# A transformer layer with adaptive layernorm: the attention gate's columns on GpSimd and VectorE instead of TensorE, its rows by way of DRAM, and four edits of order

## The chip, the core and the metric

The kernel runs on one core of one Trainium2 chip. TensorE (PE, with its weight loads shown as PEld) multiplies 128x128 weights with a moving tile of up to 512 columns into PSUM, eight banks of 512 fp32 columns on 128 partitions. VectorE (DVE), ScalarE (ACT) and GpSimd (POOL) work on SBUF, the first two on PSUM too. Nearly all transfers, among them the transposing ones ("turns"), are issued in order by SyncE (SP), and the FFN's gate and up weights by ScalarE. Each engine has its own instruction stream and waits on semaphores. The metric is the device time of one execution in microseconds (us), given as the median of several runs.

## The reference

Sequence 2048, model width 1024, 32 query heads and 4 key/value heads of width 128, a window of the last 512 keys, FFN width 3584, inputs in bf16. Six modulation vectors of 1024 come from a condition `c`.

```
mod = silu(c) @ w_mod                      # [1, 6*1024]: sa, ca, ga, sb, cb, gb
h = layernorm(x) * (1 + ca) + sa
q = h @ wq                                 # 32 heads
o = softmax(q @ k.T / sqrt(128)) @ v       # last 512 keys, 8 query heads per key head
x = x + ga * (o @ wo)
h = layernorm(x) * (1 + cb) + sb
out = x + gb * ((silu(h @ w_gate) * (h @ w_up)) @ w_down)
```

The change concerns `ga` (the attention gate: its 1024 values and the row of them that multiplies the attention output), the row of `gb`, the row of `silu(c)` that the later modulation columns are made with, and some of the order.

## The kernel before

All work is written from one Python body through a tracker (`T.op`), which knows the last writer and the readers of each buffer and puts the needed semaphore waits in front of an instruction. So the order on every engine is the order of the code, and nothing is reordered later. SBUF is one arena in which stages share space by hand; a new use of a region absorbs the waits of the old one.

**Opening (to L742).** x is loaded in chunks of 512 rows (4 tiles of 128). Chunk 0 is normalized and turned by PE. The columns of `ca` and `sa` are made on PE by products with one moving column (`mod_mm`, into bank XB = 7), and heads 0 to 7 of chunk 0 are projected before `sa` is known. `q_raw` keeps these projections in fp32, `q_bias_mm` makes the missing `sa @ wq` per head on PE, and `q_shifted` (L666) adds it. `shift` (L671) adds `sa` to chunk 0 for all later heads. Keys are turned by four PE transposes per key head (`k_turn`) and evicted by `k_evac`, the first in the opening, the others in steps 2, 4 and 6.

**Attention (L839 to L912).** A loop over `i` runs over 4 chunks x 32 heads. One step issues on PE: the query projection of head i + 3 (eight 512-column products into bank QB, evicted at L640; half a projection in steps 1 to 8), the scores of head i - 1 (four 512-column products, two exponentials on ScalarE), and the product with the values of head i - 2 (16 products of 129 columns). VectorE takes the reciprocal of the sums (L775), multiplies (L778), and SP turns the result into `oT_all`. `run_bg(1)` then advances a list of background tasks by one turn: `ln_task`, the layernorm of a later chunk (statistics at L415, powers on GpSimd at L420 and L422, `norm` at L426, an SP turn, `modulate` at L431), and `row_task`. Loads are issued at fixed steps: `LOADO` (output weights), `LOADX`, `load_wq`, `LOADT`. When a chunk's heads are done, `oproj` runs eight output pieces of 32 products, each followed by `resid` (L797, L799) with the gate's row `rowb[0]`.

**The gate.** `load_wga` brings the 1024x1024 part of `w_mod` in two halves (steps 2 and 3). In steps 7 (four weight chunks) and 9 to 12 (one each) `mod_mm` makes the 8 columns of `ga` on PE, 8 products of one column for each chunk. `row_task` turns columns into a row on all partitions: GpSimd makes diagonal tiles (L600), PE multiplies ones by four of them into XB, VectorE evicts (L608); twice. It runs three times: for `ga` from step 12, for `silu(c)` from step 17, and for `gb` once the 24 later columns are done. These later columns are made by VectorE (`mod_col`, L585) from SP turns of `w_mod` and the row of `silu(c)`.

**FFN (L915 on).** For each chunk 28 pairs of gate and up products, then `down`: eight pieces of 512 columns (the last of chunk 3 is two of 256), `resid` with `rowb[1]` and a store.

Of the kernel before, what the change touches and what calls it, by code (L numbers as in the profile page):

```python
# [3 lines left out]
ALU = mybir.AluOpType  # L4
# [3 lines left out]
P = 128  # L8
# [122 lines left out]
def bass_adaLN_cond__sliding_block_cached__swiglu_ffn__prompt_kernel(  # L131
# [53 lines left out]
    c6 = S_("c6", [P, DT], F32)  # L185
    mcol = S_("mcol", [P, 3 * DT], F32)
    gain = [S_("gain%d" % i, [P, DT], BF16) for i in range(2)]
# [24 lines left out]
    B_ident = _Buf("ident"); B_ones = _Buf("ones"); B_zw = _Buf("zw")  # L212
    B_diag = [_Buf("diag%d" % i) for i in range(4)]
    ident = arena.at(OFF_H20, [P], BF16, [B_ident])
    ones_bf = arena.at(OFF_H20 + 256, [P], BF16, [B_ones])
    diag = [arena.at(OFF_H20 + 512 + 256 * i, [P], BF16, [B_diag[i]]) for i in range(4)]
# [17 lines left out]
    B_cT = _Buf("cT"); B_sc = _Buf("sc"); B_late = [_Buf("late%d" % i) for i in range(4)]; B_c6 = _Buf("c6"); B_mcol = _Buf("mcol"); B_scr = _Buf("scr")  # L234
# [23 lines left out]
    with nc.Block() as block:  # L258

        @block.gpsimd  # L260
        def _(g):
# [32 lines left out]
            T.op(POOL, lambda: g.memset(ones_bf, 1.0), writes=[B_ones])  # L294
            T.op(POOL, lambda: g.memset(mhalf[:, :], -0.5), writes=[B_mh])
            T.op(POOL, lambda: g.memset(zwarm, 0.0), writes=[B_zw])  # L296

# [205 lines left out]
            T.op(ACT, lambda: A.activation(sc_bf[:, :], bank_bf(XB)[:, 0:DT], AF.Silu), writes=[PB[XB], B_sc])  # L503
            T.op(ACT, lambda: A.activation(acc[:, 0:1], mhalf[:, 0:1], AF.Exp), reads=[B_mh], writes=[B_acc])
# [54 lines left out]
            GCOLS = [(j, j) for j in range(DT)]  # L559

# [33 lines left out]
            def row_task(dst, dbuf, src, sbuf):  # L594
                T.op(POOL, lambda: g.tensor_copy(c6[:, :], src), reads=[sbuf], writes=[B_c6])

                def diags(n):
                    for q in range(4):
                        col = 4 * n + q
                        T.op(POOL, lambda: g.tensor_scalar(diag[q], ident, c6[:, col:col + 1], None, op0=ALU.mult),  # L600
                             reads=[B_ident, B_c6], writes=[B_diag[q]])

                diags(0)
                yield
                for n in range(2):
                    for q in range(4):
                        mm(bank(XB, P, q * P), ones_bf, diag[q], q == 0, q == 3, [B_ones, B_diag[q]], PB[XB], skip=True)
                    T.op(DVE, lambda: V.tensor_copy(dst[:, n * 512:(n + 1) * 512], bank(XB)),  # L608
                         writes=[PB[XB], dbuf])
                    if n == 0:  # L610
                        diags(1)
                    yield


# [117 lines left out]
            q_raw(6)  # L732
            mod_sa(3)
            T.op(DVE, lambda: V.tensor_copy(mod_bf[:, 0:DT], psap(XB * 512, [[2, DT]])), writes=[PB[XB], B_mode])
            qproj_mm(7, QB0[7], 0, HK)
            q_bias_mm(0, 2, BB)
            q_shifted(0)
            qproj_mm(7, QB0[7], HK, DT)
# [8 lines left out]
            oT_all = arena.at(OFF_OT, [Hq, CH], BF16, B_oT)  # L747

# [79 lines left out]
            def add_ln2(ch):  # L828
                s = ch % 2
                if ch == 0:  # L830
                    finish(rows)
                    h2s[0] = arena.at(OFF_H20, [DT, CH], BF16, B_h2[0])
                ln2[ch] = ln_task(ch, h2s[s], B_h2[s], 1, 3 * DT, B_late[1])
                bg.append(ln2[ch])

            LOADX = {19: 2, 40: 3}
            LOADT = {Hq + 2 + (9 * n) // 4: n for n in range(NL)}
            LOADO = {5 + (21 * p) // 8: p for p in range(8)}
            for i in range(1, NA + 2):  # L839
# [11 lines left out]
                for gk in {2: (1,), 4: (2,), 6: (3,)}.get(i, ()):  # L851
                    k_turn(gk, XB)
                    kd, ks = k_evac(gk, XB)
                    T.op(DVE, lambda: V.tensor_copy(kd, ks), writes=[PB[XB], B_kT[gk]])  # L854
                    if gk == Hkv - 1:
                        for b_ in B_hT[1]:
# [205 lines left out]
```

## Time and profile before

| | |
|---|---|
| median of 3 runs | 1274.79 us (1274.72 to 1275.56) |
| profiled execution | 1274.48 us, its span 1272.6 us |
| PE busy | 1259.1 us of the span |
| VectorE / ScalarE / GpSimd busy | 479.6 / 341.5 / 42.0 us |
| one-column products on PE from `sc_bf` | 192, of which 64 for the gate |
| row products on PE, 128x128 | 24, 2.3 us busy |
| HBM read and written | 119.54 MB, 4.19 MB |

The span is the time from the first to the last recorded instruction. "Busy" is the union of an engine's instructions; matmuls overlap, so the duration of one in the timeline is longer than the distance between two. In a line of the timeline the columns are start, duration (both us), engine, line, operation, output <- inputs, shapes and count; brackets at the end give the idle time before it and what ended it. Lines that a helper issues carry the helper's number: all products stand at L268, all PE transposes at L272.

### The profile page before, as it was taken

The numbers are of one execution on the slowest core, as the hardware profiler recorded it, in microseconds if no ns is written. First come the engines' busy times: TensorE is split into PE (matmuls) and PEld (weight loads), VectorE is DVE, ScalarE is ACT, GpSimd is POOL, SyncE is SP. The second block draws the span as 40 slices with busy tenths as digits, with TensorE's granted clock in tenths as the row PEclk, the third lists the DMA queues.
The fourth block names the chain that finished last, engine by engine and source line by source line (L and its number), as shares of the span: only waits on it lengthen the run. The fifth ranks groups of instructions, "written<-read, shape, count | busy, mean of one in ns | idle before, by whom it ended". The sixth has DMA issues, their size and how long they took to land.

```text
span 1272.6 us, 17800 instructions
## 1 busy us (share of the span) xinstructions
PE 1259.1 (99%) x7541; PEld 645.7 (51%) x7683; DVE 479.6 (38%) x897; ACT 341.5 (27%) x388; POOL 42.0 (3%) x102
## 2 busy tenths in 40 slices
PE   8999999999999999999999999999999999999999
PEld 5655545555455564455544444444444444444444
DVE  4655315764147651365322321233212331222122
ACT  4655204554025550155510111011100111011100
POOL 1020000000000010000000000000000000000000
PEclk9999999999999999999999999999999999999999
DMA  9999304886028641055353973055411644035200
GB/s 317 276 227 220 96 1 90 191 168 132 1 43 186 136 108 34 5 130 121 65 145 99 289 226 114 25 157 149 153 54 61 187 141 133 17 123 159 66 9 25
DMA packets 235854, 155.31 MB, mean 122 GB/s; under 512 B 129024, under 2 KB 222080, under 8 KB 235776
## 3 DMA queue, kind: packets, MB, share of 16 engines
q1 hardware_dynamic: 177520, 95.45, 31.2%
q10 hardware_dynamic: 58256, 58.73, 14.6%
q8 instruction: 60, 0.98, 0.3%
q14 instruction: 18, 0.15, 0.0%
HBM read 119.54 MB, written 4.19 MB: 97 GB/s over the span
## 4 chain that ended last, share of the span: by engine, by line
PE 98%; issue 1%; DVE 1%; POOL 0%; POOLq 0%
PE ps L268 98%; PE ps L272 0%; DVE arena L671 0%; DVE arena L666 0%; DVE rl L775 0%; DVE arena L778 0%; DVE arena L640 0%; DVE st L415 0%; POOL arena L296 0%; DVE tmp L797 0%; DVE arena L799 0%; DVE arena L487 0%; DVE arena L854 0%; POOL arena L291 0%; DVE bq L661 0%
## 5 line engine op out<-in xcount | busy, mean ns | idle before, releaser
L268 PE MATMUL ps<-arena 128*128 128x512 bf16 (+2 forms) x7236 | 1251.7, 333 | 10.3 <-POOL arena L408 2.2
L268 PEld LDWEIGHTS ps<-arena 128*128 128x128 bf16 x7378 | 635.5, 98 | 618.7 <-issue 2.2
L757 ACT ACTIVATE arena<-ps 128x1024 bf16<-128x1024 f32 x256 | 261.9, 1023 | 349.6 <-PE ps L268 337.8
L991 ACT ACTIVATE arena<-ps 128x512 bf16<-128x512 f32 x112 | 66.9, 597 | 506.4 <-PE ps L268 506.4
L992 DVE TENSOR_TENSOR arena<-ps,arena 128x512 bf16<-128x512 f32 x112 | 77.4, 691 | 276.6 <-PE ps L268 276.6
L797 DVE TENSOR_TENSOR tmp<-ps,rowb 128x512 f32<-128x512 f32 (+1 forms) x65 | 44.4, 683 | 318.8 <-PE ps L268 318.8
L640 DVE CAST arena<-ps 128x512 bf16<-128x512 f32 x120 | 82.9, 691 | 52.3 <-PE ps L268 52.3
L778 DVE TENSOR_TENSOR arena<-ps,rl 128x512 bf16<-128x512 f32 x128 | 88.5, 691 | 4.7 <-DVE rl L775 0.3
L775 DVE RECIPROCAL rl<-ps 128x4 f32<-128x4 f32 x128 | 23.3, 182 | 119.0 <-PE ps L268 118.9
L415 DVE BATCH_NORM_STATS2 st<-x_res 128x6 f32<-128x512 bf16 x62 | 42.3, 683 | 3.5 <-DMA x_res<-in_A_x_dram 3.4
L420 POOL TENSOR_SCALAR rstd<-mv 128x1 f32<-128x1 f32 x28 | 6.3, 226 | 887.2 <-DVE mv L419 887.2
L585 DVE SCALAR_TENSOR_TENSOR arena<-arena 128x1024 bf16<-128x1024 bf16 x24 | 29.1, 1214 | 0.0
L799 DVE TENSOR_TENSOR arena<-tmp,x_res 128x512 bf16<-128x512 f32 (+1 forms) x33 | 22.3, 675 | 1.1
L799 DVE TENSOR_TENSOR x_res<-tmp,x_res 128x512 bf16<-128x512 f32 x32 | 22.1, 692 | 1.1
L431 DVE TENSOR_SCALAR arena<-arena,gain,mod_bf 128x512 bf16<-128x512 bf16 x56 | 20.3, 405 | 0.0
L426 DVE TENSOR_SCALAR nsc<-x_res,mv,rstd 128x1024 bf16<-128x1024 bf16 x30 | 16.0, 534 | 0.0
L422 POOL TENSOR_TENSOR rstd<-rstd,mhalf 128x1 f32<-128x1 f32 x28 | 15.8, 563 | 2.3
L600 POOL TENSOR_SCALAR arena<-arena,c 128x128 bf16<-128x128 bf16 x24 | 14.4, 616 | 32.7 <-PE ps L268 32.4
L268 PEld LDWEIGHTS ps<-sc_bf,arena 128*128 128x128 bf16 x192 | 6.7, 96 | 2.6 <-DMA arena<-in_w_mod_dram 0.3
L268 PE MATMUL ps<-sc_bf,arena 128*128 128x1 bf16 x192 | 6.8, 163 | 0.1
L419 DVE BATCH_NORM_AGGREGATE mv<-st 128x2 f32<-128x12 f32 x28 | 5.8, 208 | 1.0
L653 DVE COPY arena<-ps 128x512 f32<-128x512 f32 x4 | 2.7, 688 | 8.2 <-PE ps L268 8.2
(53 smaller groups left out, 50.8 us busy)
## 6 DMA issues: line engine op xcount, KB each, us to landing
arena<-in_A_wq_dram SPq DMA_DIRECT2D x31, 1024.0 KB, 6.1
arena<-in_B_w_gate_dram ACTq DMA_DIRECT2D x28, 1024.0 KB, 5.3
arena<-in_B_w_up_dram ACTq DMA_DIRECT2D x28, 1024.0 KB, 8.1
arena<-in_A_wo_dram SPq DMA_DIRECT2D x8, 1024.0 KB, 6.6
arena<-in_B_w_down_dram SPq DMA_DIRECT2D x7, 1024.0 KB, 8.1
out_dram<-arena SPq DMA_DIRECT2D x15, 256.0 KB, 2.0
x_res<-in_A_x_dram SPq DMA_DIRECT2D x3, 1024.0 KB, 6.5
arena<-in_w_mod_dram SPq DMA_DIRECT2D x8, 256.0 KB, 5.6
```

Of the source, the lines that this page charges most:

```text
L268: T.op(PE, lambda: TE.matmul(out_ap, lhsT, rhs, start=start, stop=stop, skip_group_check=skip), reads=reads, writes=[bank_buf])
L415: T.op(DVE, lambda: V.bn_stats(st_[sl][:, hf * 6:hf * 6 + 6], x_res[:, t, hf * 512:hf * 512 + 512]), reads=[B_x[t]], writes=[B_st[sl]])
L431: T.op(DVE, lambda: V.tensor_scalar(dst[:, dt, :], dst[:, dt, :], gain[gi][:, dt:dt + 1], mod_bf[:, ccol + dt:ccol + dt + 1], op0=ALU.mult ...
L585: T.op(DVE, lambda: V.scalar_tensor_tensor(mt[n % 2], mt[n % 2], 1.0, sc_row, op0=ALU.mult, op1=ALU.mult, accum_out=mcol[:, n:n + 1]), rea ...
L640: T.op(DVE, lambda: V.tensor_copy(qT_s[qs], bank(b)), writes=[PB[b], B_qT[qs]])
L757: T.op(ACT, lambda: A.activation(ex_s[es][:, 2 * kp:2 * kp + 2, :], banks2(SCB + 2 * kp), AF.Exp, scale=att_scale), writes=[PB[SCB + 2 * k ...
L775: T.op(DVE, lambda: V.reciprocal(rl[r][:, :].rearrange("p (a b) -> p a b", a=2), psap(PVB * 512 + P, [[512, 2], [130, 2]])), writes=both + ...
L778: T.op(DVE, lambda: V.tensor_tensor(o_s[os_].rearrange("p (a b) d -> p a b d", a=2), psap(PVB * 512, [[512, 2], [130, 2], [1, P]]), rlb, A ...
L797: T.op(DVE, lambda: V.tensor_tensor(tmp[s][:, 0:n], bank(b, n), rowb[ri][:, c0:c0 + n], ALU.mult), reads=[B_row[ri]], writes=[PB[b], B_tmp ...
L799: T.op(DVE, lambda: V.tensor_tensor(dst[:, c0:c0 + n], tmp[s][:, 0:n], x_res[:, t, c0:c0 + n], ALU.add), reads=[B_tmp[s], B_x[t]], writes= ...
L991: T.op(ACT, lambda: A.activation(sg_s[ss], bank(gb), AF.Silu), writes=[PB[gb], B_sg[ss]])
L992: T.op(DVE, lambda: V.tensor_tensor(guT[:, ft, :], bank(ub), sg_s[ss], ALU.mult), reads=[B_sg[ss]], writes=[PB[ub], B_gu[ft]])
```

## The change

- **Gate columns.** `mod_mm` for the gate is gone. `gate_part` computes on GpSimd, in fp32, weight chunk times `silu(c)` of its partition, added up over chunks 0 to 4, in halves of 512 columns (18 operations, written out after steps 4 to 15). `gate_row` does chunks 5 to 7 on VectorE, one `scalar_tensor_tensor` of 1024 columns at the end of steps 19, 20 and 21. The sum over the 128 partitions is left: `gate_split` (GpSimd) writes the fp32 sum as two bf16 parts, `gate_turn` (SP, steps 23 and 24) turns each, and `gate_sum` (VectorE, steps 26 and 27) reduces each turned part along the free axis; the two are added into `mstg`.
- **Rows.** `row_task` is gone. `row_turn` (SP) turns the 128x128 tile `mstg`, so that the 8 columns become 8 partitions; `row_put` writes them as one row of 1024 to a DRAM scratch, and `row_get` reads the row onto all partitions. `ga`: steps 28, 30, 31. `gb`: steps 90, 92, 93. `silu(c)`: no turn, since ScalarE makes it in row form in the opening (`c_sil`); steps 33 and 35.
- **Order.** The copy of the `sa` columns stands ahead of `q_raw(6)`, and the first bias products after two chunks of head 7's projection instead of four. The key turns of steps 2, 4 and 6 stand behind the scores. The layernorm of chunk 1 is added in step 7 instead of 5.
- **Last pieces.** The last 512 columns of the last tile are split 384 and 128 instead of 256 and 256.

```diff
-            T.op(POOL, lambda: g.memset(ones_bf, 1.0), writes=[B_ones])
             T.op(POOL, lambda: g.memset(mhalf[:, :], -0.5), writes=[B_mh])
             T.op(POOL, lambda: g.memset(zwarm, 0.0), writes=[B_zw])
+            T.op(POOL, lambda: g.memset(mstg, 0.0), writes=[B_mstg])
...
+            T.op(ACT, lambda: A.activation(c_sil, c_row[:, :], AF.Silu), reads=[B_cT], writes=[B_csil])
...
+            def row_put(r, src, sbuf):
+                T.op(Q_dr[r], lambda: SP.dma_start(d_rows[r:r + 1, :].rearrange("o (k p) -> (o k) p", p=P), src),
+                     reads=[sbuf], writes=[B_dr[r]])
+
+            def row_turn():
+                T.op(Q_turn, lambda: SP.dma_start_transpose(mrow.rearrange("p (a b) -> p a b", a=1), mstg),
+                     reads=[B_mstg], writes=[B_mrow])
+
+            def row_get(r, dst, dbuf):
+                rep_ap = bass.AP(tensor=d_rows.tensor, offset=r * D, ap=[[0, P], [1, D]])
+                T.op(Q_rw[r], lambda: SP.dma_start(dst, rep_ap), reads=[B_dr[r]], writes=[dbuf])
...
-            q_raw(6)
             mod_sa(3)
             T.op(DVE, lambda: V.tensor_copy(mod_bf[:, 0:DT], psap(XB * 512, [[2, DT]])), writes=[PB[XB], B_mode])
-            qproj_mm(7, QB0[7], 0, HK)
+            q_raw(6)
+            qproj_mm(7, QB0[7], 0, 2)
             q_bias_mm(0, 2, BB)
             q_shifted(0)
-            qproj_mm(7, QB0[7], HK, DT)
+            qproj_mm(7, QB0[7], 2, DT)
...
+            NGP = 5
+            g_acc = arena.at(OFF_OT + 28 * KB, [D], F32, B_ga)
+            g_tmp = arena.at(OFF_OT + 16 * KB, [512], F32, [B_gx])
...
+            def gate_part(n):
+                k, hf = divmod(n, 2)
+                a = g_acc[:, hf * 512:(hf + 1) * 512]
+                w = wga[:, k, hf * 512:(hf + 1) * 512]
+                if k == 0:
+                    T.op(POOL, lambda: g.tensor_scalar(a, w, sc_bf[:, k:k + 1], None, op0=ALU.mult),
+                         reads=[B_wga[k], B_sc], writes=[B_ga[hf]])
+                else:
+                    T.op(POOL, lambda: g.tensor_scalar(g_tmp, w, sc_bf[:, k:k + 1], None, op0=ALU.mult),
+                         reads=[B_wga[k], B_sc], writes=[B_gx])
+                    T.op(POOL, lambda: g.tensor_tensor(a, a, g_tmp, ALU.add), reads=[B_gx], writes=[B_ga[hf]])
...
+            def gate_row(k):
+                T.op(DVE, lambda: V.scalar_tensor_tensor(g_acc, wga[:, k, :], sc_bf[:, k:k + 1], g_acc, op0=ALU.mult, op1=ALU.add),
+                     reads=[B_wga[k], B_sc], writes=B_ga)
+
+            def gate_split():
+                T.op(POOL, lambda: g.tensor_copy(g_part[0], g_acc), reads=B_ga, writes=[B_gp[0]])
+                T.op(POOL, lambda: g.tensor_tensor(g_part[1], g_acc, g_part[0], ALU.subtract),
+                     reads=B_ga + [B_gp[0]], writes=[B_gp[1]])
+
+            def gate_turn(i):
...
+                T.op(Q_gt[i], lambda: SP.dma_start_transpose(g_turn[i], g_part[i]), reads=[B_gp[i]], writes=[B_gt[i]])
...
+            def gate_sum(i):
+                T.op(DVE, lambda: V.tensor_reduce(gsum[:, i * DT:(i + 1) * DT], g_turn[i], mybir.AxisListType.X, ALU.add),
+                     reads=[B_gt[i]], writes=[B_gsum])
+                if i == 1:
+                    T.op(DVE, lambda: V.tensor_tensor(mstg[:, 0:DT], gsum[:, 0:DT], gsum[:, DT:2 * DT], ALU.add),
+                         reads=[B_gsum], writes=[B_mstg])
...
+            GATEP = {4: (0, 1), 5: (2,), 6: (3,), 7: (4,), 9: (5,), 10: (6,), 12: (7,), 13: (8,), 15: (9,)}
+            GATER = {19 + n: NGP + n for n in range(DT - NGP)}
+            GATET = {23: 0, 24: 1}
+            GATES = {26: 0, 27: 1}
+            t2 = Hq + 6 + (9 * (NL - 1)) // 4
+            TURNT = (28, t2 + 1)
+            PUTT = {33: (0, c_sil, B_csil), 30: (1, mrow[0:DT, :], B_mrow), t2 + 3: (2, mrow[0:DT, :], B_mrow)}
+            GETT = {35: (0, sc_row, B_scr), 31: (1, rowb[0][:, :], B_row[0]), t2 + 4: (2, rowb[1][:, :], B_row[1])}
...
-                if i == 17:
-                    bg.append(row_task(sc_row, B_scr, sc_bf[:, :], B_sc))
-                if i == 5:
+                if i == 7:
                     add_ln1(1)
...
-                for k in {7: (0, 1, 2, 3), 9: (4,), 10: (5,), 11: (6,), 12: (7,)}.get(i, ()):
-                    mod_mm(wga[:, k, :], B_wga[k], k, GCOLS)
...
                 if 1 <= i - 1 < NA:
                     scores(i - 1)
+                for gk in {2: (1,), 4: (2,), 6: (3,)}.get(i, ()):
+                    k_turn(gk, XB)
+                    kd, ks = k_evac(gk, XB)
+                    T.op(DVE, lambda: V.tensor_copy(kd, ks), writes=[PB[XB], B_kT[gk]])
...
                 run_bg(1)
+                for n in GATEP.get(i, ()):
+                    gate_part(n)
+                if i in GATER:
+                    gate_row(GATER[i])
+                if i == max(GATER):
+                    gate_split()
...
-                    pieces[-1:] = [(TPC - 1, 512, 256), (TPC - 1, 768, 256)]
+                    pieces[-1:] = [(TPC - 1, 512, 384), (TPC - 1, 896, 128)]
```

## The prediction

> **What bounds the kernel now.** I read the page's busy times and its chain first. TensorE (PE) is busy for 99% of the span, its clock is granted at nine tenths or more in all forty slices, and the chain that ended last is PE for 98%.
>
> ```profile
> PE 1259.1 (99%) x7541; PEld 645.7 (51%) x7683; DVE 479.6 (38%) x897; ACT 341.5 (27%) x388; POOL 42.0 (3%) x102
> ...
> PE 98%; issue 1%; DVE 1%; POOL 0%; POOLq 0%
> ```
>
> So time can be won only by taking instructions off PE or closing its few waits. The timeline shows both. The reciprocal L775 starts when a head's second product ends, once a step, so the distance of two of them is the length of a step.
>
> ```profile
> 50.19 0.18 DVE L775 RECIPROCAL rl<-ps 128x4 f32<-128x4 f32 x1 [1.57 <-PE ps L268]
> ...
> 52.83 0.18 DVE L775 RECIPROCAL rl<-ps 128x4 f32<-128x4 f32 x1 [0.67 <-PE ps L268]
> ...
> 56.52 0.18 DVE L775 RECIPROCAL rl<-ps 128x4 f32<-128x4 f32 x1 [1.28 <-PE ps L268]
> ...
> 71.11 0.18 DVE L775 RECIPROCAL rl<-ps 128x4 f32<-128x4 f32 x1 [1.08 <-PE ps L268]
> ...
> 74.83 0.18 DVE L775 RECIPROCAL rl<-ps 128x4 f32<-128x4 f32 x1 [1.08 <-PE ps L268]
> ...
> 82.05 0.18 DVE L775 RECIPROCAL rl<-ps 128x4 f32<-128x4 f32 x1 [1.08 <-PE ps L268]
> ...
> 85.54 0.18 DVE L775 RECIPROCAL rl<-ps 128x4 f32<-128x4 f32 x1 [1.08 <-PE ps L268]
> ```
>
> A plain step takes 3.495 us (78.55 to 85.54 are two; the last is shown), and step 8, with half a projection, 2.64 (50.19 to 52.83). Step 9, with 8 gate products, takes 3.69, and step 14, with one half of a row task, 3.72 (71.11 to 74.83). The excess is the price on PE.
>
> Two waits of PE lie in the early steps:
>
> ```profile
> 31.69 0.38 PE L272 MATMUL ps<-arena 128*128 128x128 bf16 x4 [0.35 <-DVE bq L661]
> ...
> 46.54 0.55 PEld L268 LDWEIGHTS ps<-arena 128*128 128x128 bf16 x4 [0.24 <-DVE arena L640]
> ```
>
> The key turn of step 2 waits for VectorE to empty bank XB. The projection of step 7 waits 0.24 us for an eviction behind the layernorm statistics that step 5 queued. GpSimd's diagonals, a norm of VectorE beside them, and the last VectorE operation follow:
>
> ```profile
> 92.01 2.61 POOL L600 TENSOR_SCALAR arena<-arena,c 128x128 bf16<-128x128 bf16 x4
> ...
> 93.36 0.54 DVE L426 TENSOR_SCALAR nsc<-x_res,mv,rstd 128x1024 bf16<-128x1024 bf16 x1
> ...
> 1270.27 0.42 DVE L799 TENSOR_TENSOR arena<-tmp,x_res 128x256 bf16<-128x256 f32 x1
> ```
>
> **The change part by part.** The profiled execution took 1274.48 us around a span of 1272.6; the median of the runs, 1274.79, is 0.31 above it. I sum against 1274.48. A change under 0.2% (2.55 us) cannot be told from none.
>
> *Gate products off PE.* 64 products of one column go. Step 9 is 0.20 over a plain step, and steps 10 to 12 are alike: 4 x 0.20 = 0.8. Step 7 has the other 32 (at 47.42). It took 3.67 (46.52 to 50.19); less the 2.64 of a half step and its 0.24 wait, they cost 0.79. Sum: 1.6 us won.
>
> *Rows off PE.* Each row task is 2 x 4 products, and a step with four of them is 0.225 longer (3.72 against 3.495). Three tasks: 6 x 0.225 = 1.35 us won. Six VectorE evictions of 0.68 and 24 GpSimd products go as well, off the path.
>
> *Early order.* The mode copy moves ahead of the 0.69 copy of q_raw(6), and the bias products come after two chunks of head 7's projection. The bias column, ready at 28.45 before, is then ready near 27.86 (bias products done at 27.5, VectorE free at 27.7, copy 0.16). PE's order follows by its own rows, 0.216 per 512-column product and 0.39 per 16 bias products: head 7's rest ends at 28.78, first scores 29.64, bias 30.03, head 8's projection 31.76 without the wait for XB, second scores 32.62, key turn (0.22) 32.84, second product (0.90) 33.74. It ended at 34.54 before: 0.80 us won. VectorE's eight additions to chunk 0 (L671, 2.19 in all) would run from 28.77 to 30.96, each ahead of the product that reads it.
>
> *Key turns behind the scores, layernorm from step 7.* In step 6 VectorE's order is then 0.48 + 0.69 + 0.42 + 0.87 = 2.46 of a step of 2.86, and the 0.24 wait goes. Next to be late there is the projection's eviction, with 0.8 us in hand. The layernorm of chunk 1 takes 19 steps; its statistics, GpSimd powers and four SP turns all move two steps, past no other use of XB or of their tiles, and it ends in step 25. Step 29 needs it, so it costs 0; finished by force there, it would put a modulation of 0.36 in front of an eviction.
>
> *Last pieces 384 and 128.* PE's sum is the same: 28 x 0.162 plus 28 x 0.056 (128x129 products run at 0.90 / 16) is 6.1 us, against 2 x 3.06. The last two VectorE operations shrink from 0.42 each; 512 columns take 0.69, so 128 take 0.285: 0.27 us won. The 384 piece needs 2 x 0.56 of VectorE, which the 1.57 of the last products covers. The stores landed in 1.7 us at 128 KB and 1.6 at 64, so the last one, 32 KB, gets 1.6 (1.5 at best).
>
> *What is added on VectorE.* Three gate rows in steps 19 to 21 (L585, 128x1024, takes 1.21) and two reductions in steps 26 and 27, put at the same 1.2. The cover is PE's step: 0.89 for the head, 1.21, then 0.69 for the eviction makes 2.8 of 3.49. Without that 0.7 of room each would cost its excess; between 0 and 0.5 a step I take 0, since mod_col already runs so (213.51) without a PE wait. The gate rows wait for GpSimd's last part; heads' evictions and then PE stand behind them.
>
> *What is added on SP.* Four turns at 1.2 and six row transfers at 0.5 to 1.0, at most two of them in a step, beside 1.2 to 2.5 of existing issue. The gate turns of steps 23 and 24 wait for GpSimd's split. It starts near 98.5; even at 2 x 4.9 us (twice the largest price below) the second turn leaves about 2.8 us late. Behind it stand the head turns (four o tiles give three steps of room) and a query-weight load that is used four steps later, 14 us for a landing of 6.1. Cost 0. Row 0 is fetched in step 31 and first read a whole output piece after step 33; the condition row is fetched in step 35 and read in step 38. Their two-hop path has 7 us or more for landings of 2 to 4. The third row is first read in the down projection.
>
> *What is added on GpSimd.* Eighteen operations on 512 columns, from the landing of the first weights near 35.8 (issue 28.92 plus 6.9). No row has this shape. Low: the 128x512 memset, 0.52. By the slope of L420 (one column, 0.226) and L600 (128 columns, 0.616): 1.8. High: four times L600, 2.46. I take 1.8, since it is the same operation. Eight must be done before the rstd of step 8, which VectorE's norm needs near 55.3: 8 x 1.8 = 14.4 of the 18.5 us there. Then four stand between two norms, 7.2 + 1.0 of 10.5. GpSimd is not late below 2.3 us; at 2.46 the norms lose about 1 us each and PE, with 1.3 of room, nearly nothing.
> The Trainium skill, GPSIMD Engine Reference, section "Performance versus the Vector engine", gives 4497 ns for an add of 2048 fp32 columns, an estimated 1.1 us for 512; no run here has such an add. By it GpSimd is early and the total stays 1270.6.
>
> *Contention.* VectorE's bias additions (q_shifted, L666) in steps 4 to 7 and norms in 9, 12 and 15 will meet a busy GpSimd. At 93.36 a norm of 0.54 ran inside L600's four: it kept its 0.54, and GpSimd took 2.61 instead of 2.39. By that row the price is 0; a gain has no source. If VectorE waited for a whole operation of 1.8 each time, room of 0.37 (step 4), 0.8 (step 6) and 1.3 (norms) leaves 1.43 + 1.0 + 3 x 0.5 = 3.9. I take 0.3, near the row, since it is the only overlap.
> SBUF — State Buffer, "Who interferes with whom", of the Trainium skill speaks against the change: the port pair of VectorE's two-port modes and GpSimd is a lock held for a whole instruction, whoever starts first. The row at 93.36 shows the delay on GpSimd's side alone; by the rule the cost would be an estimated 2 and more, and the total near 1272.6.
>
> The ACT operation on the condition row falls into ACT's idle 1.17 us before L508; the first warm products may start 0.15 earlier, but the norm that ends at 10.25 sets the end there: 0.
>
> Sum: 1.6 + 1.35 + 0.80 + 0.24 + 0.27 - 0.3 = 3.96 won, 1274.48 - 3.96 = 1270.5; against the median 1270.8. I say **1270.6**.
>
> **The rivals.**
> 1. *GpSimd is the new bound (slower).* Above 2.4 us an operation, rstd is late and VectorE stands in the norm with the projection's eviction behind it. The cost is about 8 x (p - 2.48) + 8 x (p - 2.37), which eats the 4 us at p = 2.68 and makes it slower by 0.2% at 2.84. At 3.1 it is 10.8, so 1281. For it: no fp32 add in the trace. Against: the slope gives 1.8.
> 2. *VectorE waits for GpSimd's port.* Up to 3.9 of the 4.3 goes: 1271.5 to 1274.2, middle 1272.7.
> 3. *The early order wins nothing,* because a load or a shift is late instead: without 0.80 it is 1271.4. The 0.3 waits for loads at 19.66 and 21.39 speak for it; the loads read after 27 were issued at 19 to 24, against it.
> 4. *The rows' detours hold up a read* (row, turn or put late): VectorE would stop, PE with it, some 2 us: 1272.6.
>
> **How the numbers follow.** Forecast 0.6, first rival 0.09, second 0.18, third 0.09, fourth 0.04. Forecast and third are faster, as are half of the second and of the fourth: 0.79. Same: the rest of those, 0.12. Slower: 0.09. The range: contention at 0, the 0.15 of the warm products and 0.1 of the last store in full, and 0.25 for the rounding of step differences give 1269.8, and the second rival's upper part without its last stretch gives 1273.3; the first rival and that stretch are left out. The forecast's own range is 1269.8 to 1271.5.
>
> **What would show it.** Right: steps 9 to 14 at 3.49, the second product of step 2 ending near 33.7, no PE wait at step 7, the last VectorE pair at 0.285 each. GpSimd's operations below 2.3 us and norms straight behind the head's multiplication would clear the first rival; bias additions late in steps 4 and 6 would show the second. Wrong: a PE wait on L640 or L666 anywhere from step 4 to 15, or steps 19 to 27 longer than 3.49.

## The result, and the profile after

| | before | after |
|---|---|---|
| median, 22 runs each | 1274.84 us (1274.29 to 1276.38) | 1272.87 us (1272.12 to 1273.94) |
| ratio, 95% interval | | 0.9984 (0.9978 to 0.9990) |
| profiled execution, its span | 1274.48, 1272.6 us | 1273.07, 1271.1 us |
| VectorE / GpSimd busy | 479.6 / 42.0 us | 485.8 / 55.9 us |

The changed kernel is 1.97 us faster, half of the 3.96 forecast and less than 0.2%. The prediction wanted 0.2% (2.55 us) to tell a change from none; with 22 runs of each kernel the interval still lies clear of 1. PE still bounds it. First, from the page of the kernel after, its busy times, the chain by engine, and GpSimd's new operations:

```profile
PE 1264.0 (99%) x7595; PEld 641.9 (50%) x7595; DVE 485.8 (38%) x897; ACT 341.6 (27%) x389; POOL 55.9 (4%) x95
...
PE 97%; DMA 2%; DVE 0%; SPq 0%; issue 0%; DVEq 0%
...
L765 POOL TENSOR_SCALAR arena<-arena,sc_bf 128x512 f32<-128x512 bf16 x8 | 12.6, 1576 | 0.5 <-POOL arena L767 0.2
...
L767 POOL TENSOR_TENSOR arena<-arena 128x512 f32<-128x512 f32 x8 | 10.1, 1265 | 0.7
```

DMA now holds 2% of the chain, where before it had no entry. The page of the kernel before has 142 products fewer than weight loads (7541 and 7683), so PE's busy times of the two pages can't be compared; the weight loads, 7683 and 7595, show the 88 products that are gone. GpSimd takes 1.58 and 1.27 us an operation. The timeline of VectorE after, with the reciprocals (L824 now) of heads 4 to 8:

```profile
46.46 0.18 DVE L824 RECIPROCAL rl<-ps 128x4 f32<-128x4 f32 x1 [0.48 <-PE ps L271]
...
49.09 0.18 DVE L824 RECIPROCAL rl<-ps 128x4 f32<-128x4 f32 x1 [1.11 <-PE ps L271]
...
51.73 0.18 DVE L824 RECIPROCAL rl<-ps 128x4 f32<-128x4 f32 x1 [0.54 <-PE ps L271]
...
55.23 0.18 DVE L824 RECIPROCAL rl<-ps 128x4 f32<-128x4 f32 x1 [1.08 <-PE ps L271]
...
58.72 0.18 DVE L824 RECIPROCAL rl<-ps 128x4 f32<-128x4 f32 x1 [0.47 <-PE ps L271]
```

Step 7 is a bare half step (2.63 instead of 3.67) and the former gate steps are plain steps (3.50 and 3.49 instead of 3.69). These terms came in as forecast. Following the same reciprocal through both traces shows where the time went. Each line below is the change in one place, after against before:

| place | change, us |
|---|---|
| loads of the opening, from run to run | +0.54 |
| early order, from the last `sa` products to head 0's reciprocal (8.46 to 7.86) | -0.60 |
| step 7: gate products and its wait | -1.04 |
| heads 7 to 10: gate products | -0.79 |
| heads 11 to 28: rows (four steps, -0.90) and step 27 (+0.05) | -0.86 |
| second output stage, after head 63 | +0.69 |
| heads 89 and 90: row | -0.45 |
| last output stage, after head 127 | +0.40 |
| last pieces | +0.6 |
| sum, as the spans have it | -1.5 |

Without the opening's loads, which scatter in every kernel, this is -2.05, close to the medians' -1.97. Two output stages and the end gave back 1.7 us. The end, in VectorE's timeline after:

```profile
1266.73 0.56 DVE L848 TENSOR_TENSOR arena<-tmp,x_res 128x384 bf16<-128x384 f32 x1
1267.70 0.29 DVE L846 TENSOR_TENSOR tmp<-ps,rowb 128x128 f32<-128x128 f32 x1 [0.41 <-PE ps L271]
1269.04 0.29 DVE L848 TENSOR_TENSOR arena<-tmp,x_res 128x128 bf16<-128x128 f32 x1 [1.04 <-DMA out_dram<-arena]
```

The last addition waits 1.04 us for a store. And PE waits twice for an SP turn, which it doesn't in the kernel before. Its timeline after, in the second output stage:

```profile
313.51 6.86 PE L271 MATMUL ps<-arena 128*128 128x512 bf16 x31 [0.52 <-DMA arena<-arena]
```

The table of waits after has this one and the one of the last output stage (us in all, times, longest):

```profile
PE ps L271 <- DMA arena<-arena: 0.7, 2, 0.5
```

The two waits shown are 0.52 and 0.23, and the stages lose 0.69 and 0.40. The 0.17 more is there each time because the record of a product reaches past the start of the next one, so a gap between two records is shorter than the time lost.

### The profile page after: what moved, and what is told of

Its sections match the earlier page's. It is cut to its first block, busy times and chain, and to the rows that moved or that the text cites. A ratio compares the mean times of both kernels' runs of the same rounds, so it can differ in the third digit from the quotient of the medians.

```text
span 1271.1 us, 17772 instructions
## 1 busy us (share of the span) xinstructions
PE 1264.0 (99%) x7595; PEld 641.9 (50%) x7595; DVE 485.8 (38%) x897; ACT 341.6 (27%) x389; POOL 55.9 (4%) x95
## 4 chain that ended last, share of the span: by engine, by line
PE 97%; DMA 2%; DVE 0%; SPq 0%; issue 0%; DVEq 0%
PE ps L271 97%; DMA arena<-arena 1%; DMA arena<-in_w_mod_dram 0%; PE ps L275 0%; SPq L309 0%; DMA out_dram<-arena 0%; DVE arena L827 0%; SPq L334 0%; DVE arena L587 0%; DVE arena L848 0%; DVE arena L490 0%; DVE arena L638 0%; DVE tmp L846 0%; SPq L582 0%; DVE rl L824 0%
## 5 line engine op out<-in xcount | busy, mean ns | idle before, releaser
L271 PE MATMUL ps<-arena 128*128 128x512 bf16 (+1 forms) x7354 | 1258.3, 334 | 3.5 <-POOL arena L298 2.0
L824 DVE RECIPROCAL rl<-ps 128x4 f32<-128x4 f32 x128 | 23.3, 182 | 112.8 <-PE ps L271 112.8
L848 DVE TENSOR_TENSOR arena<-tmp,x_res 128x512 bf16<-128x512 f32 (+2 forms) x33 | 22.3, 676 | 2.1 <-DMA out_dram<-arena 1.0
L429 DVE TENSOR_SCALAR nsc<-x_res,mv,rstd 128x1024 bf16<-128x1024 bf16 x30 | 19.2, 641 | 0.0
L765 POOL TENSOR_SCALAR arena<-arena,sc_bf 128x512 f32<-128x512 bf16 x8 | 12.6, 1576 | 0.5 <-POOL arena L767 0.2
L767 POOL TENSOR_TENSOR arena<-arena 128x512 f32<-128x512 f32 x8 | 10.1, 1265 | 0.7
```

The costliest lines, as they stand in the source:

```text
L271: T.op(PE, lambda: TE.matmul(out_ap, lhsT, rhs, start=start, stop=stop, skip_group_check=skip), reads=reads, writes=[bank_buf])
L824: T.op(DVE, lambda: V.reciprocal(rl[r][:, :].rearrange("p (a b) -> p a b", a=2), psap(PVB * 512 + P, [[512, 2], [130, 2]])), writes=both + ...
L848: T.op(DVE, lambda: V.tensor_tensor(dst[:, c0:c0 + n], tmp[s][:, 0:n], x_res[:, t, c0:c0 + n], ALU.add), reads=[B_tmp[s], B_x[t]], writes= ...
```

## The experiments

The questions were the last pieces (1, 2, 12), the parts by themselves (3, 4), the waits for the turns (5 to 9), GpSimd (10) and whether the losses can be covered (11, 12). The edits are shown shortened: calls without the tracker's wrapping, and `...` where lines are left out. Medians stand beside those of the kernel before on the same chip.

**1. The last pieces alone** (on the kernel before).

```diff
-pieces[-1:] = [(TPC - 1, 512, 256), (TPC - 1, 768, 256)]
+pieces[-1:] = [(TPC - 1, 512, 384), (TPC - 1, 896, 128)]
```

> The kernel before with the last pieces 384 and 128 alone. Theory A (the last addition, which writes the same row tile as the piece before, waits until that piece's store has landed): the tail is longer, not shorter. In the changed kernel the last multiplication starts at 1267.70 and the span ends at 1271.1, 3.4 us; before it was 1269.81 to 1272.6, 2.8 us. So about 0.6 us slower than before, near 1275.4, with a wait of about 1 us in front of the last addition. Rival B (the tail is shorter, as forecast, and what is missing was lost to loads and turns that landed late): 0.27 us faster, 1274.6. The opening and the output stages are those of before, so their waits show what a kernel without the new DMA has.

1275.60 against 1274.87, ratio 1.0007 (0.9998 to 1.0016): the interval takes in 1, so the cost is read from the ends of the two traces. Its end, in VectorE's timeline:

```profile
1270.63 0.29 DVE L797 TENSOR_TENSOR tmp<-ps,rowb 128x128 f32<-128x128 f32 x1 [0.41 <-PE ps L268]
1271.99 0.29 DVE L799 TENSOR_TENSOR arena<-tmp,x_res 128x128 bf16<-128x128 f32 x1 [1.06 <-DMA out_dram<-arena]
```

The wait comes with the split. Both pieces are written into one row tile, and the tracker knows tiles, not columns. The addition of the last piece is a write of a tile that the store of the 384 piece still reads, so it waits until that store has landed. With 256 and 256 no such wait is there, and the time from the last multiplication to the end of the span was 2.8 us (1269.81 to 1272.6); here it is 3.4. The last multiplication of the kernel before:

```profile
1269.81 0.42 DVE L797 TENSOR_TENSOR tmp<-ps,rowb 128x256 f32<-128x256 f32 x1 [2.17 <-PE ps L268]
```

**2. The last piece in a tile of its own** (on the kernel after; `y_s[0]` has been free for long).

```diff
-resid(b, t, c0, n, 1, k, y_s[t % 4], B_y[t % 4])
-q = t % 4
+q = 0 if last and k == len(pieces) - 1 else t % 4
+resid(b, t, c0, n, 1, k, y_s[q], B_y[q])
```

> The changed kernel, with the last 128 columns written to another row tile (that of t = 12, whose store is long done), so that the last addition has no store to wait for. Theory A: the 1.04 us wait goes and the span ends 1.0 us earlier: near 1271.9, 3.0 below before. Rival B: the store's end only moves behind the other store, and the time stays at 1272.9.

1272.11 against 1274.87, ratio 0.9981 (0.9972 to 0.9990), 0.76 less than the kernel after. VectorE's timeline:

```profile
1267.17 0.29 DVE L846 TENSOR_TENSOR tmp<-ps,rowb 128x128 f32<-128x128 f32 x1 [0.41 <-PE ps L271]
1267.50 0.29 DVE L848 TENSOR_TENSOR arena<-tmp,x_res 128x128 bf16<-128x128 f32 x1
```

The addition follows at once, and the end comes 2.4 us after the multiplication (span 1269.6) instead of 3.4. So the shared tile is the cause.

**3. The order alone** (on the kernel before: mode copy and bias early, key turns behind the scores, layernorm in step 7).

```diff
...
-            q_raw(6)
             mod_sa(3)
...
-            qproj_mm(7, QB0[7], 0, HK)
+            q_raw(6)
+            qproj_mm(7, QB0[7], 0, 2)
...
-                if i == 5:
+                if i == 7:
                     add_ln1(1)
```

> The kernel before with the order edits alone: mode copy ahead of q_raw(6), bias products after two chunks, key turns behind the scores, layernorm of chunk 1 from step 7. Forecast by the prediction: 0.80 + 0.24 = 1.04 us faster, 1273.8. From the profile after (PE waits 0.16 us for the mode copy, and steps 0 to 4 gained 0.6 over the opening): 0.84, so 1274.0. If a load is what the opening waits for (rival 3): 0.24 only, 1274.6.

1274.59 against 1274.87, ratio 0.9998 (0.9989 to 1.0007). PE's weight loads in its timeline show a new wait in step 29:

```profile
124.74 0.10 PEld L268 LDWEIGHTS ps<-arena 128*128 128x128 bf16 x1 [0.52 <-DVE arena L431]
125.06 1.99 PEld L268 LDWEIGHTS ps<-arena 128*128 128x128 bf16 x21 [0.23 <-DVE arena L431]
```

With `row_task` still among the background tasks, the layernorm that starts two steps later is not done by step 29 and is finished there by force. Step 29 takes 3.81 us, 0.31 more than a plain step, and the order's gain (0.60 in the opening and 0.24 in step 7) is partly lost to that. In the kernel after `row_task` is gone, and the wait is not there.

**4. Gate and rows alone** (the kernel after with the old order, the layernorm in step 5 and 256/256).

```diff
...
-                if i == 7:
+                if i == 5:
                     add_ln1(1)
...
-                    pieces[-1:] = [(TPC - 1, 512, 384), (TPC - 1, 896, 128)]
+                    pieces[-1:] = [(TPC - 1, 512, 256), (TPC - 1, 768, 256)]
```

> The changed kernel with the order and the tail of before: only the gate columns and the rows are moved off PE. Forecast by the prediction: 1.6 + 1.35 = 2.95 us faster than before, 1271.9; steps 9 to 14 at 3.495. With the layernorm from step 5, VectorE's statistics and its waits for GpSimd's port meet in steps 5 to 7, so the 0.24 us wait of step 7 may grow to 1: 1271.9 to 1272.7. If the new DMA (turns, puts, gets) or the later end of GpSimd's work delays o turns or loads in general (rival C), half of the 2.95 is lost again at the output stages: 1273.3.

1273.85 against 1274.87, ratio 0.9992 (0.9984 to 1.0001). It wins 1.02 where the prices on PE add up to 2.95. The wait for the turn is there (0.3 us, the stage after head 63 takes 7.34), and the early layernorm now meets the gate's rows, in VectorE's timeline:

```profile
99.32 1.28 DVE L773 SCALAR_TENSOR_TENSOR arena<-arena,sc_bf 128x1024 f32<-128x1024 bf16 x1
100.52 0.68 DVE L638 CAST arena<-ps 128x512 bf16<-128x512 f32 x1
101.47 0.18 DVE L824 RECIPROCAL rl<-ps 128x4 f32<-128x4 f32 x1 [0.27 <-PE ps L271]
101.69 0.69 DVE L827 TENSOR_TENSOR arena<-ps,rl 128x512 bf16<-128x512 f32 x1
102.30 2.09 DVE L434 TENSOR_SCALAR arena<-arena,gain,mod_bf 128x512 bf16<-128x512 bf16 x2
104.30 0.68 DVE L638 CAST arena<-ps 128x512 bf16<-128x512 f32 x1
```

A modulation pair of 2.09 beside GpSimd's split pushes the eviction to 104.30, and PE waits 0.3 for VectorE once (steps 22 and 24 are 0.12 and 0.29 longer). So the parts lean on each other: the later layernorm keeps clear of the gate rows only where the row task is gone. The three parts alone add to -0.28 - 1.02 + 0.73 = -0.57, against -2.0 together. These two clashes account for about 0.7 of the difference; the rest lies within the three intervals.

**5 to 7. The new transfers, one kind at a time** (on the kernel before). If they held up the turns at the output stages, one of these shows it.

```diff
+if i in (30, 33, 92): SP.dma_start(d_rows[r:r + 1, :].rearrange("o (k p) -> (o k) p", p=P), c_row[:, :])
```

> The kernel before with nothing changed but three more transfers on SP, each of eight partitions (the condition row, 2 KB) to a DRAM scratch that nothing reads, at steps 30, 33 and 92. The three kernels with the new rows landed the turn of head 63 5.6, 5.3 and 5.5 us after its issue and that of head 127 after 9.3, 9.3 and 9.2; the three without landed them after 4.4, 4.7, 4.1 and 8.3, 7.8, 8.4. Theory P (a short transfer to DRAM, which uses only part of the 16 engines, leaves all later turns later): 5.5 and 9.3 here, a PE wait of 0.2 to 0.6 us at the second and last output stage, 1275.3. Theory Q (it is the added turns, or the moment at which the stage comes): 4.4 and 8.2, 1274.9.

```diff
+if i in (23, 24): SP.dma_start_transpose(rowb[1], rowb[0])
+if i in (28, 88): SP.dma_start_transpose(rowb[1][:, 0:P], rowb[0][:, 0:P])
```

> The kernel before with four more turns on SP, two of 128x1024 in steps 23 and 24 and two of 128x128 in steps 28 and 88, whose result is overwritten before it is read. Theory Q' (the added turns shift how later turns fall on the DMA engines): the turns of heads 63 and 127 land after 5.5 and 9.3 us, and PE waits 0.2 to 0.6 us at the second and last output stage. Theory P (the short transfers) or R (the earlier moment): 4.4 and 8.2, 1274.9.

```diff
+if i in (31, 35, 88): SP.dma_start(rowb[1][:, :], bass.AP(tensor=w_mod.tensor, offset=r * D, ap=[[0, P], [1, D]]))
```

> The kernel before with three more transfers on SP, each a row of 1024 read from DRAM onto all 128 partitions (steps 31, 35 and 88), whose result is overwritten before it is read. The short puts alone and the turns alone left the turns of heads 63 and 127 at 4.2 and 8.1, and 4.0 and 7.9 us. Theory G (it is the broadcast reads): 5.5 and 9.2, and PE waits of 0.2 to 0.6 at the two output stages. Theory R (none of the new transfers; the earlier moment of the stage, or their sum): 4.2 and 8.1.

Puts 1274.92 against 1274.89, ratio 1.0001 (0.9991 to 1.0011). Turns 1274.78 against 1274.89, 0.9999 (0.9989 to 1.0009). Reads 1274.60 against 1274.78, 0.9999 (0.9989 to 1.0009). The stage after head 63 takes 6.91, 6.90 and 6.91 us, as before, and PE waits for no turn. None of the three kinds by itself is the cause.

**8. The products dropped, no transfer added** (on the kernel before; its expectation says what is left out).

```diff
-mod_mm(wga[:, k, :], B_wga[k], k, GCOLS)
...
-mm(bank(XB, P, q * P), ones_bf, diag[q], q == 0, q == 3, [B_ones, B_diag[q]], PB[XB], skip=True)
+V.memset(dst[:, 0:D], 1.0)
```

> The kernel before without the gate's column products and without the products, diagonals and evictions of the three rows; a VectorE memset of ones writes each row in their place, so the output leaves out the attention gate, the FFN gate and the factor of the later modulation columns. No new transfer, no GpSimd work, order and tail as before. The prediction's price of the products: 1.6 + 1.35 = 2.95 us less, 1271.9. Theory R (a stage that comes 3 us earlier meets the loads otherwise and its turn lands later): the turns of heads 63 and 127 at 5.5 and 9.2, PE waits of about 0.5 and 0.3, so 2.1 less: 1272.7. If the turns land at 4.2 and 8.1, the waits are due to the new transfers together, and the whole 2.95 shows.

1273.68 against 1274.78, ratio 0.9990 (0.9981 to 1.0000). The table of waits:

```profile
PE ps L268 <- DMA arena<-arena: 0.9, 2, 0.5
```

Nothing was added, and the wait appears: taking products off PE is what makes the turn late. The median doesn't decide it, since it lies above both forecasts (1271.9 and 1272.7) and the runs scatter from 1272.63 to 1275.28; in the profiled one, the slowest, the loads of the opening came 2.0 us later than before. By the places of the trace the products' 2.94 is won, and 0.64 and 0.60 are lost at the two output stages.

In all traces instructions arrive in 16 KB blocks on a queue of their own (q8, 59 or 60 blocks a run). That they are PE's is read from their spacing. Where PE makes only 512-column products (0.216 each) they come about 27.6 us apart, which is 128 products with their weight loads. Where the attention steps run, 28 products in 3.495 us, 128 products take 16.0 us, and most blocks come 13 to 19 us apart. So the place of a block goes with the count of PE instructions. A block is one transfer, which takes 1.07 to 1.15 us in the median of each trace (0.9 to 2.3 in all). The 88 products that are gone (64 and 24) are about two thirds of a block. The transfers in a window of 7 us from the reciprocal of head 63, before:

```profile
q1 hardware_dynamic: 2630, 1.43, 83.9%
q14 instruction: 1, 0.01, 0.3%
...
arena<-in_w_mod_dram SPq DMA_TRANSPOSE x1, 5.6
arena<-arena SPq DMA_TRANSPOSE x1, 4.4
```

and the same window after:

```profile
q1 hardware_dynamic: 2638, 1.44, 100.4%
q8 instruction: 1, 0.02, 0.9%
...
arena<-in_w_mod_dram SPq DMA_TRANSPOSE x1, 6.5
arena<-arena SPq DMA_TRANSPOSE x1, 5.6
```

The columns of the first lines are packets, MB and the share of 16 engines; the last number of the others is the time from issue to landing. Nearly the same traffic, one block of PE's instructions more, and the two turns land 0.9 and 1.2 us later. Over all kernels with the products in their places (before and experiments 1, 3, 5 to 7) head 63's turn lands 4.0 to 4.7 us after its issue and head 127's 7.7 to 8.4. In all without (after and experiments 2, 4, 8, 10 to 12) it is 5.2 to 5.6 and 9.1 to 9.5, and the block starts 2.2 to 3.3 us after head 63's reciprocal and 3.2 to 4.6 after head 127's, while the turn is under way. With the products in place the nearest blocks start 7.9 to 8.6 us ahead of head 63's reciprocal and 9.1 to 9.4 behind it, and 9.7 to 10.3 behind head 127's, so none falls into a turn.

The other heads' turns show the same. For 34 of the heads 36 to 127, some of the 14 traces of this case start a block within 2 us of the issue of that head's turn, and others don't. The turn then lands later by 1.2 us in the median of these heads, and by 0.7 to 1.7 in the middle eight tenths of them. How a block of about 1 us does this isn't shown: the traces don't say which DMA engine carries it. In the windows above the packets of the same traffic take more time together (100.4% against 83.9).

**9. Forty products given back** (on the kernel after: ten products of one column in each of steps 40 to 43, which nothing reads). This moves the blocks and adds only 1.0 us of work to PE.

```diff
+if i in (40, 41, 42, 43):
+    for n in range(10):
+        mm(bank(XB, 1, 2 * n), ident, sc_bf[:, 0:1], n == 0, n == 9, [B_ident, B_sc], PB[XB], skip=True)
```

> The changed kernel with forty one-column products on PE that nothing reads, ten each in steps 40 to 43. Theory I: PE's instruction stream is loaded in blocks of 16 KB (60 blocks, 0.98 MB, in the profile before, 27.6 us apart where products take 0.216, so 128 products each), and a block takes one DMA engine for about 1.05 us. In the seven kernels without the 88 products a block starts 2.2 to 3.3 us after the reciprocal of head 63 and 3.2 to 4.6 after that of head 127, while the turn of that head is under way; in the six kernels with them it starts after the landing, at 9.1 and 9.7 or later. Forty more products put both blocks some forty products earlier, ahead of the turns' issue: the turns land after 4.3 and 8.1 us again, PE does not wait for them, 0.8 us is won against 1.0 us for the products (0.2 for eight): 1273.1. Rival: the block is a coincidence and it is something else in the shorter program; landings stay at 5.5 and 9.2, the waits stay, 1273.9.

1272.78 against 1274.74, ratio 0.9985 (0.9975 to 0.9994). The forty products cost 0.25 us in each of four steps, 1.0 in all, and the time is that of the kernel after: the price came back. The window of 7 us from head 63's reciprocal:

```profile
q1 hardware_dynamic: 2633, 1.43, 76.6%
...
arena<-in_w_mod_dram SPq DMA_TRANSPOSE x1, 5.1
arena<-arena SPq DMA_TRANSPOSE x1, 4.3
```

The blocks now start 3.5 and 4.0 us ahead of the two reciprocals, the turns land in 4.3 and 8.1, the stage is back at 6.90, and PE waits for no turn. What was won is the 0.69 and 0.40 of the table, 1.09 for 1.0 spent.

**10. GpSimd's multiplications three times** (on the kernel after).

```diff
 else:
-    T.op(POOL, lambda: g.tensor_scalar(g_tmp, w, sc_bf[:, k:k + 1], None, op0=ALU.mult), ...)
+    for _ in range(3):
+        T.op(POOL, lambda: g.tensor_scalar(g_tmp, w, sc_bf[:, k:k + 1], None, op0=ALU.mult), ...)
```

> The changed kernel with each product of gate chunks 1 to 4 on GpSimd made three times over into the same tile, so that a part takes about 6.3 us of GpSimd instead of 3.0. Prediction's first rival (GpSimd late, VectorE stands in the norm, the projection's eviction behind it): parts 0 to 4 end near 60 instead of 51, the norm of step 9 starts 4.8 us late and PE, with 1.3 of room, waits 3.5; norms 12 and 15 are late by 3.0 each. In all 9.5 us: 1282.4. If GpSimd's work is hidden whatever its length: 1272.9.

1284.34 against 1274.89, ratio 1.0075 (1.0056 to 1.0093), 11.5 above the kernel after. VectorE's timeline:

```profile
60.34 0.92 DVE L429 TENSOR_SCALAR nsc<-x_res,mv,rstd 128x1024 bf16<-128x1024 bf16 x1 [4.26 <-POOL rstd L425]
...
73.76 0.92 DVE L429 TENSOR_SCALAR nsc<-x_res,mv,rstd 128x1024 bf16<-128x1024 bf16 x1 [2.04 <-POOL rstd L425]
...
87.24 0.92 DVE L429 TENSOR_SCALAR nsc<-x_res,mv,rstd 128x1024 bf16<-128x1024 bf16 x1 [3.79 <-POOL rstd L425]
```

VectorE stands ahead of the norm for GpSimd's rstd, three times, 10.1 us in all, and the steps around the three norms are 5.1, 1.2 and 4.7 us longer. The first rival's mechanism is real. It was expected to cost 9.5. At the measured size it is far off: in the kernel after no norm waits for rstd in these steps.

**11. The losses covered** (experiment 2, and: the `w_mod` turn that stands just ahead of head 63's turn one step later, 28 products of the last output stage ahead of the wait for head 127's turn, and the bias after three chunks).

```diff
+LOADT = {Hq + 2 + (9 * n) // 4 + (n == 14): n for n in range(NL)}
...
-qproj_mm(7, QB0[7], 0, 2)
+qproj_mm(7, QB0[7], 0, 3)
...
+oproj_mm(NCH - 1, 3, SCB + 1, 0, HL)
-for k, b in enumerate((QB, XB, SCB)):
+for k, b in enumerate((QB, XB, SCB, SCB + 1)):
...
-for k, b in ((3, SCB + 1), (4, QB), (5, XB), (6, SCB + 2), (7, QB)):
+for k, b in ((4, QB), (5, XB), (6, SCB + 2), (7, QB)):
```

> The changed kernel with four edits: the last 128 columns in a row tile of their own (as in the kernel with the freed tail); the w_mod turn of step 65, which is issued right in front of head 63's turn, one step later; the first 28 products of output piece 3 ahead of the four last heads of pieces 0 to 2 in the last output stage; the bias products after three chunks of head 7 instead of two. Expected by the waits in the profile after: 0.8 for the tail, 0.5 and 0.3 for PE's waits for the turns of heads 63 and 127, 0.16 for the mode copy: 1272.9 - 1.8 = 1271.1, no PE wait for a turn. If the waits only move to another place: 1272.1, as with the freed tail alone.

1270.85 against 1274.89, ratio 0.9970 (0.9958 to 0.9981): 4.04 us faster than the kernel before, 2.0 faster than the change, the fastest here. The blocks fall where they fall in the kernel after and the turns still land in 5.4 and 9.1. But head 63's turn is issued 0.94 us after its reciprocal instead of 1.48, since the `w_mod` turn now stands behind it, and ahead of head 127's PE has other work: the stage after head 63 takes 6.90 and no product waits for a turn. From the last `sa` products to head 0's reciprocal it is 7.73 instead of 7.86.

**12. The same with pieces of 256 and 256.**

```diff
-pieces[-1:] = [(TPC - 1, 512, 384), (TPC - 1, 896, 128)]
+pieces[-1:] = [(TPC - 1, 512, 256), (TPC - 1, 768, 256)]
```

> The kernel with the freed tail and the covered turns (1270.85), with the last pieces back at 256 and 256; the last one still has a row tile of its own. The prediction's price of 384 and 128 without a wait for the store is 0.27: 1271.1 here. If the size of the last piece is worth nothing once the tile is free: 1270.85; if the smaller store costs more at the end: 1270.6.

1270.98 against 1274.78, ratio 0.9971 (0.9960 to 0.9983). From the last multiplication to the end of the span it is 2.8 us, with 384 and 128 in tiles of their own 2.4: 0.4 won by the profiles, 0.13 by the medians, too little for these runs to tell from nothing.

## Why the prediction was right and wrong

The 1272.87 lies inside the stated range, 1269.8 to 1273.3, but by luck. The range reached that far only for the second rival, PE waiting behind VectorE for GpSimd's port, and that cost nothing. The forecast's own range, up to 1271.5, was missed: 2.0 of the 3.96 us are not there. By the places of the trace 1.1 of them went at two output stages that no term and no rival named, 0.9 into the last pieces, which lost 0.6 instead of winning 0.27, and 0.2 into the early order; 0.3 came back that had been taken off for contention.

- **Gate products (1.6) and rows (1.35): right where they stand.** The gate gave 0.80 + 0.79, the rows 0.86 + 0.45, with the 0.05 that step 27 took back. **What they set off was not in the sum, nor in any rival.** With 88 products fewer, blocks of PE's instructions load while the turns of heads 63 and 127 are under way, and the output stages lose 0.69 + 0.40. The fourth rival looked for a late transfer at the rows' own reads; no wait stands there in the trace after. Experiment 8 shows that the products' absence suffices, experiment 9, which has all the new transfers and no wait, that it is the count of instructions and not the work.
- **"Last pieces 384 and 128 ... 0.27 us won": wrong in sign, 0.6 to 0.7 lost.** The failed step is "the 384 piece needs 2 x 0.56 of VectorE, which the 1.57 of the last products covers". The cover held for VectorE's work, but the addition of the last piece also waits until the store of the 384 piece, which reads the same row tile, has landed. Before, PE took 3.06 us for the second piece, longer than the 1.6 in which the first one's store lands; it takes only 1.57 for 128 columns. With a tile of its own the term has the right sign: 0.4 by the profiles, 0.13 by the medians.
- **Early order (0.80): mis-sized, 0.60.** The failed step is "bias products done at 27.5": the sum let them follow two chunks at once. They wait for the mode copy. It did move ahead of the copy of `q_raw(6)`, but it must wait for the end of the `sa` products. In the old order it started 0.81 us after the start of the last of them, and in the new one 0.75 after. PE's and VectorE's timeline before:

```profile
26.28 0.54 PE L268 MATMUL ps<-sc_bf,arena 128*128 128x1 bf16 x16
...
27.09 0.15 DVE L734 CAST mod_bf<-ps 128x8 bf16<-128x8 f32 x1
```

  and after, where the new edge is seen:

```profile
26.82 0.54 PE L271 MATMUL ps<-sc_bf,arena 128*128 128x1 bf16 x16
...
27.57 0.17 DVE L731 CAST mod_bf<-ps 128x8 bf16<-128x8 f32 x1 [4.73 <-PE ps L271]
...
27.78 0.47 PEld L271 LDWEIGHTS ps<-mod_bf,arena 128*128 128x128 bf16 x16 [0.47 <-DVE mod_bf L731]
```

  PE's weight loads stand 0.47 for the copy after two chunks, and PE itself loses 0.14: the two products from 27.22 to 27.79 take 0.57 instead of 0.43. So the bias column came 0.31 earlier, not 0.59, and PE's second bias products 0.09 earlier, not 0.27. The rest of the 0.60, 0.51, lies behind them, where the wait for XB is gone, as forecast. The third chunk of experiment 11 wins 0.13.
- **The 0.24 wait of step 7: right.** The step is 2.63.
- **Contention (0.3 taken): the cost was 0, and for another reason than given.** VectorE does wait for GpSimd. In the two engines' timeline after:

```profile
54.44 1.59 POOL L765 TENSOR_SCALAR arena<-arena,sc_bf 128x512 f32<-128x512 bf16 x1
56.05 1.61 DVE L429 TENSOR_SCALAR nsc<-x_res,mv,rstd 128x1024 bf16<-128x1024 bf16 x1
56.11 1.26 POOL L767 TENSOR_TENSOR arena<-arena 128x512 f32<-128x512 f32 x1
57.58 0.68 DVE L638 CAST arena<-ps 128x512 bf16<-128x512 f32 x1
```

  The norm, 0.54 before, takes 1.61 and ends 0.29 after GpSimd's addition, which ends at 57.37; the norms of steps 12 and 15 take 1.60. The row at 93.36, where it kept its 0.54, was one overlap and misled me. That VectorE waits fits what the Trainium skill, SBUF — State Buffer, section "Who interferes with whom", states of the shared port, that one engine is blocked while the other holds it; on this the page was right and my reading of the row wrong. Which of the two came first, and whether the wait lasts for the whole addition, these rows don't show: the recorded starts are 0.06 apart. The eviction behind the norm comes at 57.58, still in time, so no PE wait follows. The second rival had the wait right and counted the step's room; it was oversized, with 1.8 for each wait. Measured are 1.07 at the norms, within their room of 1.3, and at most 0.27 at the bias additions (0.48 to 0.70 instead of 0.43 to 0.48), within 0.37.
- **GpSimd (1.8 an operation taken): 1.58 and 1.27 measured.** GpSimd was early, as forecast. An addition of 512 columns takes 1.27; the estimate of 1.1 from the Trainium skill, GPSIMD Engine Reference, section "Performance versus the Vector engine", is below that by more than a tenth. The weights landed later than the 35.8 of the prediction: 6.9 was the median of the two loads, and the first alone took 8.5 (28.92 to 37.46), so 1.7 of the 18.5 us were missing. Experiment 10 bears out the first rival's mechanism, its formula only in part. There a multiplication and its addition become three and one. By the pitches of the timeline after (1.64 from 41.00 to 42.64 and 1.37 from 42.64 to 44.01) these take 6.29, so p is 3.15 for each of two places. The formula then gives 11.6 and 11.5 was measured, but that is luck: of the first eight operations the two of chunk 0 were not repeated. With these at 1.64 the first norm's part is 2.3 and not 5.4, where the trace lost 5.1; 1.3 of the difference is the late start (37.13 and not 35.8), the rest stays open. For the two later norms the formula gives 6.2 together, and the trace lost 6.0.
- **The covers of VectorE and SP: right but for 0.05 us.** Steps 19 to 26 stayed at 3.50 us with the gate rows at 1.27 and the first reduction at 1.21 in them. Step 27, where the second reduction and the addition of the two parts (0.17) stand ahead of the eviction, took 3.54.

Added up: 0.60 + 0.24 + 1.59 + 1.31 - 1.09 - 0.6 = 2.05, against 1.97 measured.

## What to carry to other kernels

When instructions leave the engine that bounds, the loading of that engine's own instructions shifts with their count, and can fall into a transfer that the engine waits for. So look at each place where the engine starts on a transfer with little to spare, and give it some work ahead of that wait. When a last piece is split, ask which store still reads the tile that the next piece writes. Do not read a rule of sharing from one overlap in which the other engine may have come second.

## What was not expected of the hardware

- PE's instructions are loaded in blocks of 16 KB, one for about 128 products with their weight loads. A block takes about 1.1 us, and a turn under way at that time lands about 1 us later (4.0 to 4.7 becoming 5.2 to 5.6 us, 7.7 to 8.4 becoming 9.1 to 9.5).
- The loads of the opening scatter by 0.8 us between profiled runs, once by 2.0: the last `sa` products start at 26.28, 27.11, 26.64 and 26.69 us in four kernels with the same opening (before, experiments 1, 5 and 6), and at 28.25 in experiment 8. An effect of half a microsecond in one profile is read between two events behind the loads, as the 8.46 and 7.86 above, and not from the start of the span.
